# The first chunk's decays spread by one rounded product of stacked high and low rows, with eight blocks of zero products in place of eleven and a new written-out order

## The chip, the cores and the metric

One core of a Trainium2 chip runs the whole program. The metric is the device time of one execution in microseconds (us); less is better. Five engines work side by side, each through its own instructions in a fixed order: TensorE (PE, products), VectorE (DVE), ScalarE (ACT), GpSimd (POOL) and SyncE (SP, which here only issues transfers). An instruction waits for what it reads, and everything behind it on its engine waits with it.

## The reference

Two stages: a gated recurrence over 768 steps (4 batches, 8 heads, chunks of 32 in the reference), and then a gated feed-forward layer over the 3072 rows that it makes.

```python
log_a = np.log(np.clip(a, 1e-06, 1.0))
for c in range(nc):
    cum = np.cumsum(log_a[:, :, sl], axis=-1)
    L = np.exp(cum[:, :, :, None] - cum[:, :, None, :]) * causal
    M = np.einsum('bhin,bhjn->bhij', Cc, Bc) * L
    y[:, :, sl] = M @ x + (C @ state) * exp(cum)
    state = exp(sum) * state + sum_j B_j x_j exp(cum_last - cum_j)
...
gate = 1.0 / (1.0 + np.exp(-(x @ w_gate)))
val = x @ w_val
return (gate * val @ w_out)
```

x has 32 columns for each head and 16 states; the layer goes 256 -> 1536 -> 256. Everything is in 32-bit floats.

## The kernel before

The sequence is cut into six chunks of 128 steps (two halves of 64). For each chunk c the recurrence is a few products: B against C (`pcb`), times the decays, against x (`py`, `mm`), plus the state that came before (`L820`, `L647`). Chunk 0 goes through it batch by batch (`FirstUnit`, four units), since nothing else can be done while the program starts; later chunks go through it in one piece (`Scan`), between the products of the layer. The layer works on the 512 columns of a chunk: `gate` and `value` (`pg`, `pv`, 12 pairs), then `proj` (`po`). Chunks 4 and 5 are done together by a scheme with fewer products (`unit`, `ux`, `uz`, `acc`).

A product of full 32-bit floats takes TensorE several passes. Most of the layer is therefore done on two rounded parts, high and low (`fp32r`), with three products of one pass each; for that each weight tile is first put into a plain form by five instructions on three engines (`split_w`: L482 and L490 on VectorE, L488 and L495 on ScalarE, L497 on GpSimd) and later cut into parts (`part_w`: L513, L515). The first ten of the first chunk's pairs use the full 32-bit weights in their projection, and the first six in their gates as well.

**How the first chunk starts.** `a0` holds the decays of the first 128 steps, one row for each (half, batch, head), 64 rows of 64. VectorE clips them to `ac` and spreads each row over 8 head places (`apart`, a row is zero but in its own head's place; rows 64 to 127 are zero). A product for each unit b with a matrix of zeros and ones (`of_unit[:, b]`, 128 x 128) copies the right row to all 64 partitions of a half (`pa`, L741, `spread`). A running product along each row (L744, the "scan", on VectorE, 512 columns) makes the decays `ab`. Times `pcb` (L691) that is `m` (L695); `m` against x is `py` and `mm` (L706), with the unit's own state sums in the same banks (L716). `sm`, `mr` (L724), `sn` (L848) are the states; `inter`, L820, adds what the first half left to the second. `xw` (L834) takes the result, and `pgv` (L962) are the first layer's products on halves of it.

Ahead of that TensorE multiplies zeros (`warm`, L237): eleven blocks of 128 columns as two products of 512 and one of 384 (`WARM`). `keep_warm` (L289) puts in further products that nobody reads ("fills", 128 columns) where the plan sees TensorE idle in the first 45 us.

**What sets the order.** The program is written as some 300 tasks of several steps. `run()` goes through them with costs for each step (`free`, the numbers in `step(...)`), and picks among the ready steps by a number. Those numbers stand in the table `DUES`, one for each step, 0 to 1246; a letter behind one says which engine takes it (`p` GpSimd, `d` VectorE, `a` ScalarE). So the table sets the order on all engines, and the order of the transfers on SP's queue. `banks` are the three rotating result banks of TensorE (`mm`): a step that takes one waits until the one three turns ago was read out.

Of the kernel before, what the change touches and what calls it, by code (L numbers as in the profile page):

```python
# [8 lines left out]
F32 = mybir.dt.float32  # L9
F32R = mybir.dt.float32r  # L10
# [3 lines left out]
ALU = mybir.AluOpType  # L14
# [121 lines left out]
}  # L136
WARM = (4, 4, 3)
PE0 = 5.6


# [40 lines left out]
def tile_ssd_then_gated_ffn(  # L181
# [11 lines left out]
    nc = tc.nc  # L193
# [4 lines left out]
    P = 128  # L198
# [1283 lines left out]
```

## Time and profile before

| | before |
|---|---|
| median of 3 runs | 345.69 us (345.6 to 346.02) |
| the profiled execution's own time | 345.54 us |
| its span in the trace | 343.7 us |
| TensorE busy | 337.9 us (98%) |
| VectorE, ScalarE, GpSimd busy | 220.2, 150.2, 180.0 us |
| 40.16 MB moved, mean | 117 GB/s |

The span is the time from the first to the last instruction of the trace; the own time, 1.84 us more, has what lies around it. Shares of busy time are means over the whole span; the prediction therefore reads stretches.

### The profile page before, as it was taken

Reading aid. Unit: us, or ns where it says so; the run is one execution under the profiler, and the core shown is the slowest. Engines: PE = TensorE matmul, PEld = TensorE weight load, DVE = VectorE, ACT = ScalarE, POOL = GpSimd, SP = SyncE. Lnnn points to the kernel's source line nnn. Section 1 sums busy time; section 2 is a strip of 40 time slices with the busy share of each in tenths; the row PEclk is TensorE's granted clock in tenths of the full one; section 3 lists DMA queues with packets and bytes.
Section 4 is the critical chain, followed back from the end, with each engine's and each line's share of the span. In section 5 each row is a group of like instructions: output and inputs, shape, how many; then the busy total and the mean of one; then the engine's idle time right before and its main releaser. Section 6 shows DMA issues by size and latency. Waiting matters only on the chain.

```text
span 343.7 us, 7948 instructions
## 1 busy us (share of the span) xinstructions
PE 337.9 (98%) x3144; PEld 261.7 (76%) x3144; DVE 220.2 (64%) x377; ACT 150.2 (44%) x277; POOL 180.0 (52%) x181
## 2 busy tenths in 40 slices
PE   8899999999999999999999999999999999999996
PEld 3474587457888888888888888888888888888885
DVE  5889978956879872456666954566064646856221
ACT  4476987124744230136411513361047557645300
POOL 4646265431646434566774545489427885355500
PEclk9999999999999999999999999999999999999999
DMA  6996899871674376476543621108123733220032
GB/s 107 180 352 209 256 272 146 162 132 35 94 159 62 90 109 159 97 139 89 145 100 102 85 76 21 63 3 297 72 36 91 240 89 110 110 61 2 0 58 67
DMA packets 100247, 40.16 MB, mean 117 GB/s; under 512 B 88754, under 2 KB 91826, under 8 KB 99570
## 3 DMA queue, kind: packets, MB, share of 16 engines
q1 hardware_dynamic: 97906, 39.39, 49.3%
q10 hardware_dynamic: 2304, 0.26, 0.5%
q8 instruction: 25, 0.41, 0.5%
q14 instruction: 12, 0.10, 0.1%
HBM read 30.00 MB, written 9.63 MB: 115 GB/s over the span
## 4 chain that ended last, share of the span: by engine, by line
PE 98%; DVE 1%; ACT 0%; issue 0%
PE pg L981 17%; PE pv L981 17%; PE ux L1121 6%; PE acc L1121 6%; PE po L1017 5%; PE po L1013 5%; PE po L1019 5%; PE po L1018 5%; PE acc L1224 5%; PE uz L1121 5%; PE pg L972 2%; PE pv L972 2%; PE po L1251 2%; PE pcb L706 2%; PE pcb L691 2%; PE pcb L647 2%
## 5 line engine op out<-in xcount | busy, mean ns | idle before, releaser
L981 PE MATMUL pg<-xh,w 128*128 128x512 f32 x168 | 59.0, 392 | 0.0
L981 PE MATMUL pv<-xh,w 128*128 128x512 f32 x168 | 58.9, 391 | 0.0
L927 POOL TENSOR_TENSOR h<-g,h 128x512 fp32r<-128x512 f32 x27 | 38.3, 1420 | 24.4 <-ACT h L925 17.2
L921 DVE TENSOR_TENSOR g<-pv,g 128x512 f32<-128x512 f32 x38 | 26.1, 688 | 30.1 <-PE pv L981 29.1
L903 ACT ACTIVATE g<-pg 128x512 f32<-128x512 f32 x47 | 28.0, 596 | 39.4 <-PE pg L981 37.2
L981 PEld LDWEIGHTS pg<-xh,w 128*128 128x128 f32 x168 | 31.5, 188 | 6.7
L981 PEld LDWEIGHTS pv<-xh,w 128*128 128x128 f32 x168 | 31.5, 188 | 6.6
L497 POOL TENSOR_TENSOR wr<-wr 128x512 int32<-128x512 int32 x18 | 20.5, 1143 | 26.8 <-ACT wr L495 13.0
L981 PE MATMUL pg<-xl,w 128*128 128x512 f32 x84 | 32.7, 389 | 0.0
L981 PE MATMUL pv<-xl,w 128*128 128x512 f32 x84 | 32.7, 389 | 0.0
L1017 PE MATMUL po<-h,w 128*128 128x512 f32 x76 | 30.8, 405 | 0.0
L1019 PE MATMUL po<-h,w 128*128 128x512 f32 x76 | 29.6, 390 | 0.0
L1018 PE MATMUL po<-h,w 128*128 128x512 f32 x76 | 29.6, 389 | 0.0
L577 DVE TENSOR_TENSOR_SCAN ab<-ab,delta 128x512 f32<-128x512 f32 x20 | 28.1, 1424 | 0.0
L925 ACT CAST h<-g 128x512 fp32r<-128x512 f32 x26 | 16.0, 619 | 24.2 <-DVE g L921 24.0
L1048 POOL TENSOR_TENSOR c<-c,c 128x512 f32<-128x512 f32 x13 | 17.2, 1326 | 17.9 <-ACT c L1176 9.2
L1048 POOL TENSOR_TENSOR h<-c,h 128x512 fp32r<-128x512 f32 x16 | 21.0, 1323 | 9.4 <-ACT h L1200 9.3
L1048 POOL TENSOR_TENSOR sw<-sw 128x128 f32<-128x128 f32 x36 | 18.9, 535 | 11.2 <-DVE sw L1048 10.2
L1028 DVE STREAM_TRANSPOSE o<-po 128x256 f32<-128x256 f32 x16 | 6.3, 430 | 21.2 <-PE po L1019 19.2
L1200 ACT CAST h<-c 128x512 fp32r<-128x512 f32 x24 | 14.9, 619 | 10.7 <-POOL c L1048 7.1
L981 PEld LDWEIGHTS pv<-xl,w 128*128 128x128 f32 x84 | 15.8, 188 | 3.2
L981 PEld LDWEIGHTS pg<-xl,w 128*128 128x128 f32 x84 | 15.8, 188 | 3.2
(197 smaller groups left out, 733.2 us busy)
## 6 DMA issues: line engine op xcount, KB each, us to landing
w_s<-sp SPq DMA_DIRECT2D x12, 512.0 KB
s<-w_s SPq DMA_DIRECT2D x12, 512.0 KB
ab<-a_z SPq DMA_DIRECT2D x10, 512.0 KB
wr<-in_moe_w_gate_dram SPq DMA_DIRECT2D x6, 512.0 KB
wr<-in_moe_w_val_dram SPq DMA_DIRECT2D x6, 512.0 KB
wr<-in_moe_w_out_dram SPq DMA_DIRECT2D x6, 512.0 KB
xn<-in_x_dram SPq DMA_DIRECT2D x5, 512.0 KB
out_dram<-o SPq DMA_DIRECT2D x144, 16.0 KB
```

The costliest lines, as they stand in the source:

```text
L497: nc.gpsimd.tensor_tensor(out=lw.bitcast(I32), in0=hw.bitcast(I32), in1=lw.bitcast(I32), op=ALU.add)
L577: nc.vector.tensor_tensor_scan(out=t, data0=t, data1=delta.rearrange("p h l -> p (h l)"), initial=0.0, op0=ALU.mult, op1=ALU.add,)
L903: nc.scalar.activation(gs[k, f], pm, AF.Sigmoid)
L921: nc.vector.tensor_tensor(out=g, in0=pm, in1=g, op=ALU.mult)
L927: engines[eng].tensor_tensor(out=hl, in0=g, in1=hh.bitcast(F32), op=ALU.subtract)
L981: nc.tensor.matmul(pm, w[:, part, kt, fs], xx[:, kt], start=(i == 0), stop=(i == 3 * NK - 1))
L1013: nc.tensor.matmul(acc, whole[NF + f // 2][:, f % 2, ms], hs[k, f], start=start, stop=stop)
L1017: nc.tensor.matmul(acc, hi, hh, start=start, stop=False)
L1018: nc.tensor.matmul(acc, hi, hl, start=False, stop=False)
L1019: nc.tensor.matmul(acc, lo, hh, start=False, stop=stop)
L1048: engines[eng].tensor_tensor(out=out, in0=in0, in1=in1, op=op)
L1121: nc.tensor.matmul(out, a[i], b[j], start=start and n == 0, stop=n == 2, skip_group_check=True)
```

## The change

Four things. (1) `a0` is loaded twice, rows 0 to 63 by SP's queue and rows 64 to 127 by ScalarE's; VectorE rounds all 128 rows to `ah`, and in the lower 64 rows subtracts the rounded value, so that they hold the remainder. `apart` then holds high rows over low rows, `of_unit` has its ones in both halves, and the product of `spread` is one of rounded operands in which the sum over the 128 rows puts high and low together again. GpSimd's clearing of `apart`'s lower half (L1280) is gone. (2) `WARM` is (4, 4): eight blocks. (3) Some steps may now go to another engine: the rounding copy of `part_w` and of `weight_sums` to GpSimd, the picking of `sm` and `mr` in the first chunk to ScalarE. (4) `DUES` is another table, with other planned start costs (`PE0`, `free`, the `spread` step's 0.35 for 1.0).

```diff
-    "": "0 1", "b0": "2", "w0": "3", "b3": "4", "b1": "5", "products0": "6 7 9 13 18", "products0_0": "8 11 28",
...
-WARM = (4, 4, 3)
-PE0 = 5.6
+WARM = (4, 4)
+PE0 = 4.7
...
-        of_b2, eye[:, :R2].rearrange("p (o b h) -> p b o h", o=2, b=NB), axis=mybir.AxisListType.X, op=ALU.add
+        of_b2, eye2.rearrange("p (o b h) -> p b o h", o=2, b=NB), axis=mybir.AxisListType.X, op=ALU.add
...
-    of_unit = hp.tile([P, NB, P], F32, tag="h8", name="of_unit")
+    head2 = const.tile([P, H], F32, name="head")
+    nc.vector.tensor_reduce(head2, eye2.rearrange("p (k h) -> p h k", h=H), axis=mybir.AxisListType.X, op=ALU.add)
+    of_unit = hp.tile([P, NB, P], F32R, tag="h8", name="of_unit")
...
-        free = {"sp": 1.0, "pe": PE0, "act": 3.5, "dve": 5.4, "pool": 4.0, "none": 0.0}
+        free = {"sp": 1.0, "pe": PE0, "act": 3.5, "dve": 4.7, "pool": 4.0, "none": 0.0}
...
-        yield step("act", ACT_SB, needs)
+        eng = yield step(("act", "pool"), (ACT_SB, 0.75), needs)
         hw, lw = halves.pop(i)
         hi, lo = parts_of(i)
-        nc.scalar.copy(hi, hw)
+        copies[eng](hi, hw)
...
+    def chosen_of(eng, out, local):
+
+        if eng == "dve":
+            return chosen(out.rearrange("p (o c) -> p o c", o=1), local.rearrange("p (o c) -> p o c", o=1), 1)
+        for g in range(NG):
+            gs = slice(g * D, (g + 1) * D)
+            nc.scalar.mul(out[:, gs], local[:, gs], of_g[:, g : g + 1])
...
-            yield step("pe", 1.0, [("a0",)], banks=1)
+            yield step("pe", 0.35, [("a0",)], banks=1)
...
-            yield step("dve", 0.21, [], [("first", 0, b)])
+            eng = yield step(("dve", "act"), (0.21, 0.45), [], [("first", 0, b)])
...
-    apart = hp.tile([P, H, L2], F32, tag="h2", name="apart")
-    nc.gpsimd.memset(apart[R2:], 0.0)
-    a0 = hp.tile([R2, L2], F32, tag="h0", name="a0")
+    apart = hp.tile([P, H, L2], F32R, tag="h2", name="apart")
+    a0 = hp.tile([P, L2], F32, tag="h0", name="a0")
     av = a.rearrange("b h s -> (b h) s")
-    nc.sync.dma_start(a0, av[:, :L].rearrange("k (o l) -> o k l", o=2))
+    for r, eng in enumerate((nc.sync, nc.scalar)):
+        eng.dma_start(a0[r * R2 : (r + 1) * R2], av[:, :L].rearrange("k (o l) -> o k l", o=2))
...
+    ah = wk.tile([P, L2], F32R, tag="sp", name="ah", bufs=1)
+    nc.vector.tensor_copy(ah, ac)
+    nc.vector.tensor_tensor(out=ah[R2:], in0=ac[R2:], in1=ah[R2:].bitcast(F32), op=ALU.subtract)
     nc.vector.tensor_tensor(
-        out=apart[:R2], in0=ac.rearrange("p (o l) -> p o l", o=1).broadcast_to([R2, H, L2]),
-        in1=head2.rearrange("p (h o) -> p h o", o=1).broadcast_to([R2, H, L2]), op=ALU.mult,
+        out=apart, in0=ah.bitcast(F32).rearrange("p (o l) -> p o l", o=1).broadcast_to([P, H, L2]),
+        in1=head2.rearrange("p (h o) -> p h o", o=1).broadcast_to([P, H, L2]), op=ALU.mult,
     )
```

The table moves most instructions of the program somewhere; the number of products is the same but for the zero products and the fills. Three places follow as the engines' instructions stand (line, operation, output and inputs by the program's names with buffer numbers, size).

TensorE at the very start, before. `pt` are the transposed B and C of a unit, `pp` the running products that the states need.

```order
L237 MATMUL warm<-warm_sb 128x512 x2
L237 MATMUL warm<-warm_sb 128x384
L756 MATMUL pt_141<-eye,bn_127 128x128
L757 MATMUL pt_141<-eye,cq_129 128x128
L741 MATMUL pa_146<-apart,of_unit 128x512
L871 MATMUL pp_154<-apb,of_row 128x256
L741 MATMUL pa_162<-apart,of_unit 128x512
L741 MATMUL pa_167<-apart,of_unit 128x512
L691 MATMUL pcb_179<-bct_148 64x128 x8
```

The same place after the change.

```order
L234 MATMUL warm<-warm_sb 128x512 x2
L284 MATMUL warm<-eye 128x128
L744 MATMUL pa_141<-apart,of_unit 128x512
L744 MATMUL pa_144<-apart,of_unit 128x512
L759 MATMUL pt_148<-eye,bn_129 128x128
L760 MATMUL pt_148<-eye,cq_131 128x128
L284 MATMUL warm<-eye 128x128 x4
L874 MATMUL pp_161<-apb,of_row 128x256
L686 MATMUL pcb_170<-bct_155 64x128 x8
L284 MATMUL warm<-eye 128x128
```

Two spreads stand ahead of the first transposes now, and fills (`warm<-eye`) between; in the whole first chunk there are 18 fills where 4 were.

VectorE from the first scan to the last `m` of the first chunk, before; `wr_131` is the first gate weight tile (w0), `wr_192` the first value tile (w1).

```order
L744 SCALAR_TENSOR_TENSOR ab_158<-pa_146,delta 128x512
L490 TENSOR_SCALAR wr_131<-wt_160 128x512
L744 SCALAR_TENSOR_TENSOR ab_158<-pa_162,delta 128x512
L744 SCALAR_TENSOR_TENSOR ab_158<-pa_167,delta 128x512
L695 TENSOR_TENSOR m_202<-pcb_179,ab_158 128x512
L744 SCALAR_TENSOR_TENSOR ab_158<-pa_195,delta 128x512
...
L695 TENSOR_TENSOR m_202<-pcb_179,ab_158 128x512 x2
L482 TENSOR_SCALAR wr_192<-wr_192 128x512
L724 TENSOR_TENSOR sm_258<-py_284,mask 128x64
L724 TENSOR_TENSOR mr_327<-mm_228,mask 128x64
L848 SCALAR_TENSOR_TENSOR sn_333<-sm_258,pp_164,mr_327 128x64
L695 TENSOR_TENSOR m_202<-pcb_179,ab_158 128x512
```

After the change (`wr_216` is w1; w0's clip, L482 before, has gone to GpSimd).

```order
L747 SCALAR_TENSOR_TENSOR ab_151<-pa_183,delta 128x512
L747 SCALAR_TENSOR_TENSOR ab_151<-pa_191,delta 128x512
L485 TENSOR_SCALAR wr_133<-wt_195 128x512
L690 TENSOR_TENSOR m_186<-pcb_170,ab_151 128x512
L727 TENSOR_TENSOR sm_275<-py_234,mask 128x64
L690 TENSOR_TENSOR m_186<-pcb_170,ab_151 128x512
L787 TENSOR_TENSOR cd_200<-bct_202,of_q 128x256
L799 TENSOR_TENSOR bd_197<-bn_129,ab_151 128x128
L727 TENSOR_TENSOR sm_275<-py_293,mask 128x64
L782 TENSOR_TENSOR bct_155<-bct_155,pp_179 128x64
L477 TENSOR_SCALAR wr_216<-wr_216 128x512
L690 TENSOR_TENSOR m_186<-pcb_170,ab_151 128x512
```

The clip of w1 still stands ahead of the last `m`, with three short instructions of other engines' work (`cd`, `bd`, `bct`) in front of it, and two `sm` behind fewer `m`.

TensorE at the seventh gate of the first chunk (`pg_6`), before; it is the first that reads the rounded parts of x and of a weight.

```order
L972 MATMUL pg_5_567<-xw_269,wr_340 128x512 x2
L972 MATMUL pv_5_584<-xw_269,wr_335 128x512 x2
L289 MATMUL pg_6_607<-eye 128x128 x3
L981 MATMUL pg_6_607<-xh_372,w_572 128x512
L981 MATMUL pg_6_607<-xl_373,w_572 128x512
L981 MATMUL pg_6_607<-xh_372,w_572 128x512 x2
L981 MATMUL pg_6_607<-xl_373,w_572 128x512
L981 MATMUL pg_6_607<-xh_372,w_572 128x512
L289 MATMUL pv_6_629<-eye 128x128
```

The four fills there are gone in the changed program; the products around them stand as they did. Further on, VectorE's four scans of chunk 1 (L577), which stood one before and three behind the read of the last value bank (`g_11`, L921), stand together ahead of it; and SP's queue takes chunk 1's `pp` loads behind its `bn` and `xn`, not ahead.

## Rows read from the trace of the kernel before

**Rows 1.** TensorE by stretch: us, busy (instructions), granted clock, DMA share, GB/s.

```profile
0.00:24.40 24.40, 21.79 (x337) 1.00 0.88 203
24.40:340.50 316.10, 316.10 (x2809) 1.00 0.48 111
```

**Rows 2.** The chain of waits, first 45 us: start, us, engine and tile.

```profile
1.09 5.04 PE warm L237 x6
...
15.52 0.61 DVE wr L482
...
17.03 0.71 PE py L289 x4
17.74 0.17 PE py L706
...
21.73 2.79 PE pgv L962 x12
24.52 1.72 PE pg L972 x4
...
41.69 0.67 PE pg L289 x6
42.36 1.39 PE pg L981 x6
43.75 0.22 PE pv L289 x2
```

**Rows 3.** VectorE in order of time, first 20 us: start, us, line, operation, tiles.

```profile
3.24 0.23 DVE L1287 TENSOR_SCALAR ac<-a 64x64 f32<-64x64 f32 x1 [0.26 <-DMA a<-in_a_dram]
...
3.63 0.68 DVE L1289 TENSOR_TENSOR apart<-ac,head 64x512 f32<-64x512 f32 x1
...
7.25 1.22 DVE L744 TENSOR_TENSOR_SCAN ab<-pa,delta 128x512 f32<-128x512 f32 x1
...
8.93 2.34 DVE L744 TENSOR_TENSOR_SCAN ab<-pa,delta 128x512 f32<-128x512 f32 x2
...
13.12 0.40 DVE L784 TENSOR_TENSOR cd<-bct,of_q 128x256 f32<-128x256 f32 x1
13.44 0.21 DVE L724 TENSOR_TENSOR sm<-py,mask 128x64 f32<-128x64 f32 x1
14.23 1.29 DVE L695 TENSOR_TENSOR m<-pcb,ab 128x512 f32<-128x512 f32 x2 [0.58 <-PE pcb L691]
15.44 0.68 DVE L482 TENSOR_SCALAR wr<-wr 128x512 f32<-128x512 f32 x1
...
16.62 0.68 DVE L695 TENSOR_TENSOR m<-pcb,ab 128x512 f32<-128x512 f32 x1
```

**Rows 4.** All engines by stretch: PE, PEld, DVE, ACT, POOL busy, clock, DMA share, GB/s.

```profile
6.10:12.00 5.90, 5.67 (x33) 2.16 (x31) 4.86 (x7) 3.44 (x12) 3.15 (x6) 1.00 1.03 115
12.00:14.20 2.20, 1.98 (x86) 1.41 (x88) 1.65 (x4) 1.27 (x7) 1.25 (x5) 1.00 0.83 238
14.20:17.00 2.80, 1.88 (x80) 1.30 (x78) 2.73 (x7) 1.56 (x7) 1.49 (x3) 1.00 1.01 205
```

**Rows 5.** SP's queue in order of time: issue, us that it took.

```profile
10.29 0.94 SPq L468 DMA_DIRECT2D wr<-in_moe_w_val_dram  x1
11.27 1.09 SPq L434 DMA_DIRECT2D xn<-in_x_dram  x2
12.41 2.42 SPq L468 DMA_DIRECT2D wr<-in_moe_w_gate_dram  x1
```

**Rows 6.** VectorE in order of time around the seventh gate.

```profile
41.19 0.68 DVE L890 TENSOR_TENSOR xl<-xw,xh 128x512 fp32r<-128x512 f32 x1
...
42.69 0.69 DVE L515 TENSOR_TENSOR w<-wr,w 128x512 fp32r<-128x512 f32 x1
```

**Rows 7.** VectorE in order of time at chunk 1's scans.

```profile
56.37 0.69 DVE L921 TENSOR_TENSOR g<-pv,g 128x512 f32<-128x512 f32 x1 [0.73 <-PE pv L981]
...
61.13 5.31 DVE L577 TENSOR_TENSOR_SCAN ab<-ab,delta 128x512 f32<-128x512 f32 x3
```

More of the change, by code (lines that the diff above doesn't have):

```diff
@@ L265, in tile_ssd_then_gated_ffn @@
     nc.vector.tensor_reduce(
-        of_b2, eye[:, :R2].rearrange("p (o b h) -> p b o h", o=2, b=NB), axis=mybir.AxisListType.X, op=ALU.add
+        of_b2, eye2.rearrange("p (o b h) -> p b o h", o=2, b=NB), axis=mybir.AxisListType.X, op=ALU.add
     )
-    head2 = const.tile([R2, H], F32, name="head")
-    nc.vector.tensor_reduce(
-        head2, eye[:R2, :R2].rearrange("p (k h) -> p h k", h=H), axis=mybir.AxisListType.X, op=ALU.add
-    )
-    of_unit = hp.tile([P, NB, P], F32, tag="h8", name="of_unit")
+    head2 = const.tile([P, H], F32, name="head")
+    nc.vector.tensor_reduce(head2, eye2.rearrange("p (k h) -> p h k", h=H), axis=mybir.AxisListType.X, op=ALU.add)
+    of_unit = hp.tile([P, NB, P], F32R, tag="h8", name="of_unit")
     nc.vector.tensor_copy(
@@ L293, in tile_ssd_then_gated_ffn @@
     engines = {"dve": nc.vector, "pool": nc.gpsimd}
-    copies = {"dve": nc.vector.tensor_copy, "act": nc.scalar.copy}
+    copies = {"dve": nc.vector.tensor_copy, "act": nc.scalar.copy, "pool": nc.gpsimd.tensor_copy}
     def task(due, name, gen):
@@ L813, in result @@
             own(self.bd, got["xn", 0][:, b], lambda i, rows: py[i][rows, NK])
-            yield step("dve", 0.21, [], [("first", 0, b)])
+            eng = yield step(("dve", "act"), (0.21, 0.45), [], [("first", 0, b)])
             self.s1 = state_of(0, "sm", 1)[:, b]
-            chosen(self.s1.rearrange("p (o c) -> p o c", o=1), py[0][:, NK:], 1)
+            chosen_of(eng, self.s1, py[0][:, NK])
             yield step("pe", 0.32, [("cd", 0, b)], [("inter", 0, b)] + [("inter", 0)] * (b == NB - 1))
@@ L825, in result @@
             self.take(1)
-            yield step("dve", 0.21, [], [("after", 0, b)], banks=-1)
+            eng = yield step(("dve", "act"), (0.21, 0.45), [], [("after", 0, b)], banks=-1)
             if ("mr", 0) not in got:
@@ L829, in result @@
             self.after = got["mr", 0][:, b]
-            chosen(self.after.rearrange("p (o c) -> p o c", o=1), py[1][:, NK:], 1)
+            chosen_of(eng, self.after, py[1][:, NK])
         def take(self, i):
@@ L1062, in weight_sums @@
             sum_up(eng, out, in0, in1, op)
-        yield step("act", ACT_SB)
+        eng = yield step(("act", "pool"), (ACT_SB, 0.7))
         parts = hp.tile([P, 2, 512], F32R, tag="r1", name=f"sp{i}")
-        nc.scalar.copy(parts[:, 0], t[:, 1])
+        copies[eng](parts[:, 0], t[:, 1])
         eng = yield step(("dve", "pool"), (DVE_SB, POOL_SB), port=True)
@@ L1278, in tile_ssd_then_gated_ffn @@
     w_s = dr.tile([NF, P, 2 * 4 * P], F32, name="w_s")
-    apart = hp.tile([P, H, L2], F32, tag="h2", name="apart")
-    nc.gpsimd.memset(apart[R2:], 0.0)
-    a0 = hp.tile([R2, L2], F32, tag="h0", name="a0")
+    apart = hp.tile([P, H, L2], F32R, tag="h2", name="apart")
+    a0 = hp.tile([P, L2], F32, tag="h0", name="a0")
     av = a.rearrange("b h s -> (b h) s")
-    nc.sync.dma_start(a0, av[:, :L].rearrange("k (o l) -> o k l", o=2))
+    for r, eng in enumerate((nc.sync, nc.scalar)):
+        eng.dma_start(a0[r * R2 : (r + 1) * R2], av[:, :L].rearrange("k (o l) -> o k l", o=2))
     az, ap = (hp.tile([NB * H, S], F32, tag=f"h{10 - i}", name=f"a{i}") for i in range(2))
     nc.scalar.activation(table, table, AF.Sigmoid)
-    ac = hp.tile([R2, L2], F32, tag="h11", name="ac")
+    ac = hp.tile([P, L2], F32, tag="h11", name="ac")
     nc.vector.tensor_scalar(out=ac, in0=a0, scalar1=1e-6, scalar2=1.0, op0=ALU.max, op1=ALU.min)
     nc.vector.memset(ac[:, :1], 0.0)
+    ah = wk.tile([P, L2], F32R, tag="sp", name="ah", bufs=1)
+    nc.vector.tensor_copy(ah, ac)
+    nc.vector.tensor_tensor(out=ah[R2:], in0=ac[R2:], in1=ah[R2:].bitcast(F32), op=ALU.subtract)
     nc.vector.tensor_tensor(
-        out=apart[:R2], in0=ac.rearrange("p (o l) -> p o l", o=1).broadcast_to([R2, H, L2]),
-        in1=head2.rearrange("p (h o) -> p h o", o=1).broadcast_to([R2, H, L2]), op=ALU.mult,
+        out=apart, in0=ah.bitcast(F32).rearrange("p (o l) -> p o l", o=1).broadcast_to([P, H, L2]),
+        in1=head2.rearrange("p (h o) -> p h o", o=1).broadcast_to([P, H, L2]), op=ALU.mult,
     )
@@ L1353, in initial @@
         yield step("none", 0.0, [], made)
-        yield step("none", 4.9, [], [("a0",)])
+        yield step("none", 4.7, [], [("a0",)])
     task(-60.0, "", initial())
```

230 rows, old and new, of the table DUES are left out of this document.

## The prediction

> **What bounds the kernel now.** I first read TensorE's busy time by stretch [rows 1]. From 24.4 to 340.5 us it is busy for all 316.10 us, and since the change keeps the number of products, that stretch can only get shorter by what in it is not needed. Before 24.4 it lacks 24.40 - 21.79 = 2.6 us, and part of its busy time there are zero products. Behind 340.5 come 3.2 us of last reads and stores, whose instructions keep their order. So the gain has to come from the first 24 us and from fills.
>
> Then I read the chain of waits [rows 2], to see what the start hangs on. It opens with 5.04 us of zero products on TensorE (from 1.09), and later leaves TensorE for VectorE's clip of a weight tile (15.52) and comes back at 17.03 with two fills; the third unit's products start at 17.74. From 21.73 on it is TensorE alone: the half products `pgv`, and from 24.52 the first full gate. Here the reader should see that TensorE is the bound from about 17 us on, and VectorE and what it waits for ahead of that.
>
> The third view is VectorE in order of time [rows 3]. The clip of the decays starts when they land (3.24), `apart` is done at 3.63 + 0.68 = 4.31, but the first scan starts only at 7.25: TensorE was still on zeros. From there to the end of the last `m`, 16.62 + 0.68 = 17.30, VectorE works nearly without a break.
>
> **The change part by part.**
>
> *The warm-up and the spread.* Eleven zero blocks took 5.04, so eight take 3.67 and end at 4.76. The one fill behind them costs a block at that pace, 0.46: TensorE can take the first spread at 5.22. `apart` must be there: two more instructions on 64 columns, each at most the 0.23 of the clip on the same columns [rows 3], move it from 4.31 to 4.77 at the latest, and GpSimd's clearing falls away. The second half of the load goes by ScalarE's queue, which has nothing else to do; it may be 0.45 late before anything notices. A product of rounded operands, one pass, is in the rows as six in 1.39, 0.23 each; the full one is 1.72 for two, 0.86 [rows 2]. That is at the fast clock. [...] So the first rounded spread costs 0.46, ends near 5.7, and the first scan starts near 5.75 instead of 7.25. The four spreads together go from 3.44 to some 1.4 us of TensorE; the fills that come in (18 for 4) fill time in which it would wait, and cost at most 0.22 each where it would not.
>
> The zero blocks and fills in the rows show the lower level for all the zeros and the higher one from the transposes at about 6 us on; the granted-clock column says 1.00 even for the first stretch [rows 1], so I go by the durations. [...]
>
> *What VectorE has to do.* From first scan to last `m`: four scans at 2.34 / 2, four `m` at 1.29 / 2, w0's second pass and w1's clip at no more than 0.68 each, and two `sm`, `cd` and two small ones that came over from GpSimd at no more than 0.40 each [rows 3]: 4.7 + 2.6 + 1.4 + 2.0 = 10.7, or about 9.4 with the short ones at half that. Before it was 17.30 - 7.25 = 10.05. The work alone would let the last `m` end at 5.75 + 9.4 = 15.2, two us sooner.
>
> *What the data allow.* But the last `m` stands behind w1's clip, and the third unit needs its x. From 6.1 to 17 the transfers fill the queues: shares 1.03, 0.83, 1.01 [rows 4]. SP issued w1 (512 KB) at 10.29, the last two `xn` (256 KB together) at 11.27, then w2, whose issue took 2.42 [rows 5]. The bytes fit: 2.2 us at 238 GB/s are w1's half megabyte, so w1 is there by about 14.3 to 15.4 (its clip began at 15.44, which is the latest), and 256 KB at 205 GB/s more take 1.25, so x is there by about 15.6 to 16.5. The change takes no bytes from ahead of these; it adds 16 KB. I take 15.0 and 16.0. Then the clip ends at 15.6 and the last `m` at 16.3, 1.0 sooner than 17.30; the third unit's products can start at 16.0, 1.7 sooner than 17.74.
>
> *To the full gates.* From 17.74 to 24.52 TensorE did 6.78 us of work that stays. Started at 16.0 it would end at 22.8; the last `m` and the clip of w2 ahead of the last `sm` (w2 lands behind x) push that back. I take 1.3, between 1.0 and 1.7: the first full gate starts near 23.2. The bounds: 0, if x lands only when it was used before (17.74), and 2.2, if it is there at 15.6. GpSimd's clip of w0 appears in no row for that engine; between the 0.68 of VectorE and the 3 us until ScalarE needs it nothing later moves, because the data wait is behind it.
>
> *The seventh gate.* Of the four fills there (0.67 + 0.22 [rows 2]) none is left: 0.89 less. They covered a real wait in part: the low half of x was ready at 41.19 + 0.68 = 41.87, the weight of the value product at 42.69 + 0.69 = 43.38 [rows 6], while TensorE without fills would have come at 41.69 and about 43.3. In the new order VectorE makes the low half of x before the half products are even read, and the weight parts stand behind the same gate's read as before, which itself moves up. So I take 0.89; if the old waits stay, 0.6.
>
> *Elsewhere.* Two rounding copies of weights and two of sums go to GpSimd, two `mr` to ScalarE. Nothing waits for them in TensorE before, and GpSimd is idle for half of the span; I cost them at nothing. If their cover goes, a copy is 1 us late once.
>
> Sum: 345.54 - 1.3 - 0.89 = 343.35 for an execution like the profiled one. That one is 0.15 under the median of the runs (345.69), so I forecast 343.5.
>
> **The rivals.**
>
> *The start gives nothing back.* x and w1 land as late as they were used. Then only the fills of the seventh gate are gone: 345.69 - 0.9 = 344.8. For it: the queues are full all through [rows 4]. Against: TensorE lacked 0.92 us in 14.2 to 17.0 and VectorE was busy for 2.73 of 2.80, so it was work, not data, that was late there.
>
> *The new order makes waits that eat the gain.* After 24.4 there was none; the table moves almost everything. One wait of 1.5 to 2.5 us, or several short ones, gives 345.0 to 346.2. For it: hardly a row keeps its neighbours. Against: VectorE, ScalarE and GpSimd have a third to a half of their time free.
>
> [...]
>
> *Slower: chunk 1's scans.* VectorE does all four in one piece ahead of the read of the last value bank. Before, three took 5.31 [rows 7], so four take up to 7.1. TensorE has two quarter projections (8 products of 0.86, 6.9) and chunk 1's own `pcb` until it needs that bank, so there is about 1 us in hand. The decays come by a broadcast load whose landing no row shows, and in the new order the first scan is wanted at about 56.37 + 0.69 + 0.8 - 2.2 = 55.7. If it lands 1 us late nothing happens; at 3.9 us late the whole gain (2.2 + 0.7) is gone and it becomes slower, by what comes on top: 347. Against: the scans waited for no transfer before.
>
> **How the numbers follow.** Forecast as summed: 0.58, with its own range 342.6 (2.2 at the start) to 344.4 (0.6 at the start, 0.6 at the seventh gate). Start gives nothing, 344.8: 0.12. Waits eat it, 345.0 to 346.2: 0.14. Clock, 343.9: 0.04. Slower, 347: 0.12. Faster by over 0.2% (under 345.0; 0.2% is about what a measurement of this kernel can tell from no change) are the first, second and fourth: 0.74. Same 0.14, slower 0.12. The range for 8 in 10 goes from 342.6 up to 345.3, which takes in the forecast, the two mild rivals and a little of the waits.
>
> **What would show it.** First scan near 5.75; TensorE's six-product records at the seventh gate with no L289 row ahead; the first full gate at 23.2, and the first half products of chunk 0 moved by the same; `py` of the third unit near 16.0 behind a wait for a transfer; and from there TensorE busy without a gap to about 338.3. It is wrong if a TensorE wait of over 0.5 us stands anywhere behind 24 us, if the first full gate starts after 24.0, or if zero-like products keep their 0.46 beyond 6.5 us.

## The result, and the profile after

| | before | changed |
|---|---|---|
| time, median of 6 runs | 345.74 us (345.33 to 346.02) | 348.46 us (346.95 to 349.94) |
| ratio, 95% interval | | 1.008 (1.0056 to 1.0104) |
| the profiled execution: its time, its span | 345.54, 343.7 | 349.94, 348.1 |
| first scan on VectorE starts | 7.25 | 6.14 |
| first full gate starts, in the order of time | 24.36 | 26.41 |
| TensorE's last product ends | 340.50 | 343.98 |

The change made the kernel 0.8% slower, and its runs spread over 3 us where those of before lie within 0.7. The profiled execution of the changed kernel is the slowest of its six, so its 4.4 us over before are more than the 2.7 us between the medians.

The waits of TensorE are where I look first. Rows: who waited for what, us in total, times, longest.

```profile
PE py L284 <- issue: 1.3, 1, 1.3
PE pgv L965 <- DMA wr<-in_moe_w_val_dram: 1.1, 1, 1.1
PE warm L234 <- DVE warm_sb L231: 1.1, 1, 1.1
PE pcb L686 <- DVE sm L727: 0.8, 1, 0.8
PE pg L984 <- DVE g L924: 0.8, 1, 0.8
```

Three of these are new: a stop with no releaser ("issue") at the third unit's fills, one ahead of a half product that is put down to a weight's transfer, and one at a gate. They stand here in the order of time on TensorE (start, duration, instructions, idle time ahead).

```profile
15.82 0.45 PE L823 MATMUL mm<-cd,sm 128*64 128x64 f32 x8
16.20 0.38 PE L284 MATMUL py<-eye 128*128 128x128 f32 x1
17.93 0.94 PE L284 MATMUL py<-eye 128*128 128x128 f32 x7 [1.35 <-issue]
...
22.20 0.45 PE L823 MATMUL mm<-cd,sm 128*64 128x64 f32 x8
23.74 1.11 PE L965 MATMUL pgv<-xw,wr 128*128 128x256 f32 x4 [1.09 <-DMA wr<-in_moe_w_val_dram]
...
25.98 0.59 PE L965 MATMUL pgv<-xw,wr 128*128 128x256 f32 x2
26.41 1.02 PE L975 MATMUL pg<-xw,wr 128*128 128x512 f32 x2
```

A product of full 32-bit floats stands in the trace as two MATMUL records, two passes (a rounded one as one: the four spreads are 8 records before and 4 in the changed kernel). The first stop splits a zero product into its two: the first pass ran at 16.20, the second at 17.93. The second pass has no operand that the first hadn't, so no data was waited for. The second stop is at an instruction that waits for a semaphore; the last transfer that this semaphore counts had landed by 22.82, and TensorE went on at 23.64, so the wait view's releaser is not what ended it.

Against before the 4.4 us of the profiled executions are made up of: the first full gate 2.05 later; from there to the seventh gate's value product 0.82 less (18.55 for 19.37; the fills are gone); from there to TensorE's end 2.25 more (299.02 for 296.77; 0.94 of it at 106.5 us, 0.86 spread over the small products `pcb<-ab,xn` of L701, the rest in pieces); and 0.93 more behind TensorE's end (4.09 for 3.16).

VectorE at the start, as in [rows 3]:

```profile
3.66 0.26 DVE L1290 TENSOR_SCALAR ac<-a 128x64 f32<-128x64 f32 x1 [0.69 <-DMA a<-in_a_dram]
3.98 0.06 DVE L1291 MEMSET ac<- 128x1 f32 x1
4.07 0.19 DVE L1293 CAST ah<-ac 128x64 fp32r<-128x64 f32 x1
4.30 0.22 DVE L1294 TENSOR_TENSOR ah<-ac,ah 64x64 fp32r<-64x64 f32 x1
4.56 0.69 DVE L1295 TENSOR_TENSOR apart<-ah,head 128x512 fp32r<-128x512 f32 x1
...
6.14 2.34 DVE L747 TENSOR_TENSOR_SCAN ab<-pa,delta 128x512 f32<-128x512 f32 x2 [0.58 <-PE pa L744]
```

The spread that the first scan waits for, on TensorE:

```profile
5.31 1.22 PE L744 MATMUL pa<-apart,of_unit 128*128 128x512 f32 x2
```

What the change does at the start works: the scans begin 1.1 us sooner. The gain is lost behind it, on TensorE.

What stops TensorE is seen by counting. These are TensorE's products (PE) and weight loads (PEld) in two stretches, from the start to the first stop and between the stops (columns: stretch, its length, busy time, instructions in it, granted clock, DMA share, GB/s).

```profile
0.00:16.58 16.58, 14.69 (x219) 1.00 0.82 135
17.92:22.43 4.51, 4.50 (x127) 1.00 0.86 241
...
0.00:16.58 16.58, 9.75 (x220) 1.00 0.82 135
17.92:22.43 4.51, 3.65 (x126) 1.00 0.86 241
```

With TensorE's own semaphore instructions (10 up to there) the first stop stands ahead of its 450th record and the second one exactly 256 records on. The transfers have a queue of their own kind for instructions; whole span, then 15 to 16 us, then 20 to 22 us:

```profile
q8 instruction: 25, 0.41, 0.5%
...
q8 instruction: 1, 0.02, 7.0%
...
q8 instruction: 1, 0.02, 4.2%
```

25 packets of 16 KB for the 6,371 records of TensorE come to 64 bytes a record, so by this estimate one packet is 256 records, as many as stand between the two stops. The trace's packets put the two fetches at 15.35 to 16.48 and 21.04 to 22.38; TensorE goes on at 17.93 and 23.64, 1.45 and 1.26 us after each. In the trace of before the fetch ends at 16.77, and there too TensorE stops at the same record, from 17.79 to 18.12, without a semaphore. So my first theory: **instructions come in blocks of 256, and TensorE stands still at a border between two blocks when it gets there before the next has come.** Records are counted from 0 below, so the borders are records 449, 705, 961 and so on. The rival is what the wait view says: **transfers**, a weight that lands late because SP issues small loads ahead of it.

### The profile page after: what moved, and what is told of

It is laid out like the page before. It is cut to its first block, busy times and chain, and to the rows that moved or that the text cites. A ratio compares the mean times of both kernels' runs of the same rounds, so it can differ in the third digit from the quotient of the medians.

```text
span 348.1 us, 7964 instructions
## 1 busy us (share of the span) xinstructions
PE 338.9 (97%) x3158; PEld 264.3 (76%) x3158; DVE 226.5 (65%) x385; ACT 145.5 (42%) x271; POOL 177.0 (51%) x181
## 4 chain that ended last, share of the span: by engine, by line
PE 87%; SPq 5%; DMA 4%; DVE 2%; issue 1%; ACT 0%; ACTq 0%; DVEq 0%
PE pg L984 16%; PE pv L984 16%; PE ux L1124 6%; PE acc L1124 5%; PE po L1020 5%; PE po L1016 5%; PE po L1021 5%; PE po L1022 5%; PE uz L1124 5%; PE acc L1227 4%; PE pv L975 2%; PE pg L975 2%; PE pcb L701 2%; DMA out_dram<-o 2%; SPq L426 2%; DMA wr<-in_moe_w_val_dram 2%
## 5 line engine op out<-in xcount | busy, mean ns | idle before, releaser
L930 POOL TENSOR_TENSOR h<-g,h 128x512 fp32r<-128x512 f32 x23 | 31.8, 1385 | 30.0 <-ACT h L928 19.9
L924 DVE TENSOR_TENSOR g<-pv,g 128x512 f32<-128x512 f32 x38 | 26.1, 686 | 19.7 <-PE pv L984 15.3
L928 ACT CAST h<-g 128x512 fp32r<-128x512 f32 x27 | 16.6, 619 | 33.2 <-DVE g L924 33.2
L1051 POOL TENSOR_TENSOR h<-c,h 128x512 fp32r<-128x512 f32 x18 | 24.2, 1354 | 9.8 <-ACT h L1203 9.7
L572 DVE TENSOR_TENSOR_SCAN ab<-ab,delta 128x512 f32<-128x512 f32 x20 | 26.3, 1352 | 0.0
L1051 POOL TENSOR_TENSOR sw<-sw 128x128 f32<-128x128 f32 x36 | 17.2, 492 | 11.2 <-DVE sw L1051 10.5
L1031 DVE STREAM_TRANSPOSE o<-po 128x256 f32<-128x256 f32 x16 | 6.3, 431 | 23.2 <-PE po L1022 23.1
L510 POOL TENSOR_TENSOR w<-wr,w 128x512 fp32r<-128x512 f32 x7 | 9.9, 1419 | 16.3 <-ACT w L508 12.8
```

Source lines behind the costliest of these rows:

```text
L572: nc.vector.tensor_tensor_scan(out=t, data0=t, data1=delta.rearrange("p h l -> p (h l)"), initial=0.0, op0=ALU.mult, op1=ALU.add,)
L924: nc.vector.tensor_tensor(out=g, in0=pm, in1=g, op=ALU.mult)
L930: engines[eng].tensor_tensor(out=hl, in0=g, in1=hh.bitcast(F32), op=ALU.subtract)
L1051: engines[eng].tensor_tensor(out=out, in0=in0, in1=in1, op=op)
```

## The experiments

Twelve kernels, 4 to 11 runs each. The starts are those of the order of time, as in the table above; "stops" are breaks of over 0.25 us between two starts on TensorE that stand at a border and are longer than the same step takes elsewhere. A break of 0.32 at record 4034 (the changed kernel, w_first, old_fills) is not one: it is the step from a long product to the burst of L701, and that step takes 0.32 in the kernel before too, at 121.2, 141.3, 188.3 and 213.4 us, where no border is.

| run | first full gate | seventh gate | TensorE's end | span | median, ratio to before (95%) | stops at records (us) |
|---|---|---|---|---|---|---|
| before | 24.36 | 42.12 | 340.5 | 343.7 | | 449 (0.33) |
| changed | 26.41 | 43.18 | 344.0 | 348.1 | 348.46, 1.0056 to 1.0104 | 449 (1.62), 705 (1.21) |
| no_fills | 26.55 | 43.31 | 348.0 | 351.1 | 351.78, 1.0152 to 1.0208 | 4289 (1.87), 5057 (2.17) |
| wide_fills | 23.88 | 40.65 | 343.3 | 346.4 | 348.12, 1.0055 to 1.0085 | 4289 (0.27), 5057 (1.43) |
| tiny | 29.36 | 46.12 | 353.1 | 356.2 | 357.94, 1.0325 to 1.0395 | 449 (0.75), 1729 (1.89), 2753 (1.36), 3521 (1.84) |
| w_first | 25.46 | 42.22 | 342.5 | 346.5 | 347.92, 1.005 to 1.0093 | 449 (1.20), 705 (0.38) |
| before_128 | 24.60 | 46.24 | 357.4 | 360.5 | 361.71, 1.0439 to 1.0497 | 1729 (1.51), 2753 (1.92), 3521 (2.07), 4545 (1.93), 5313 (1.59) |
| before_32 | 24.54 | 43.51 | 341.9 | 345.0 | 346.70, 1.0026 to 1.0056 | none over 0.25 |
| wide_48 | 24.10 | 42.52 | 342.5 | 346.3 | 348.15, 1.0058 to 1.0127 | none behind 24 us |
| spread_only | 25.65 | 43.41 | 341.8 | 344.9 | 346.99, 1.0031 to 1.0073 | none behind 24 us |
| wide_cut | 24.23 | 41.05 | 341.5 | 345.4 | 347.01, 1.0031 to 1.0058 | 449 (0.42) |
| wide_cut_dve | 23.89 | 40.72 | 340.3 | 344.2 | 345.71, 1.0003 to 1.0023 | 449 (0.66) |
| old_fills | 24.05 | 40.82 | 339.9 | 343.0 | 345.01, 0.9977 to 1.0009 | none |
| tail | 23.64 | 41.72 | 343.7 | 346.8 | 346.77, 1.0024 to 1.0051 | none |

**no_fills.** The changed kernel without its zero products of the first chunk.

```diff
-        for _ in range(int(FILL * idle[0] / FILL_T + (0.9 if first_y[0] else MORE))):
+        for _ in range(0):
```

> The changed kernel without its 18 zero products of the first chunk (72 of TensorE's records: a weight load and a product for each of two passes). Two theories for its two stops, 16.58 to 17.93 and 22.43 to 23.74. Instructions: TensorE's instructions come from memory in blocks of 256; the 449th and the 705th record stand at these stops in the changed kernel, and each goes on 1.26 to 1.45 us after a fetch of 16 KB has landed. Then without the fills some 50 records more of useful work stand ahead of the first stop and 72 ahead of the second; the stops stand at the same record numbers, 449 and 705, at other products, and the first full gate starts at 24.5 to 25.7 instead of 26.58; 346.5 to 347.8 us. Transfers: the stop before the half products is the wait for a weight that lands late; the fills take no time from that, the wait stays in front of the same product, and the first full gate starts at 26.3 to 26.7; 348 to 349 us.

Neither came. There is no stop at 449 or 705, but the first full gate is as late as before the edit, because TensorE was slow all the way to it. Products of the same shape between 5 and 24.5 us, first in the changed kernel and then without fills (count, busy, mean ns):

```profile
L686 PE MATMUL pcb<-bct 32*64 32x128 f32 x64 | 1.9, 292 | 0.8 <-DVE sm L727 0.8
L759 PE MATMUL pt<-eye,bn 128*128 128x128 f32 x4 | 1.3, 316 | 0.0
```

```profile
L686 PE MATMUL pcb<-bct 32*64 32x128 f32 x64 | 2.9, 442 | 0.1
L759 PE MATMUL pt<-eye,bn 128*128 128x128 f32 x4 | 1.8, 445 | 0.6 <-ACT bct L769 0.6
```

So it is the fills that bring the clock to its upper level this early: the trace's first clock record, at the upper level, stands at 23.75 us without them and at 6.44 in the changed kernel. And two stops of 1.87 and 2.17 us appear at 189 and 214 us, far from the edit: in the small `pcb` products of chunks 4 and 5, at records 4289 and 5057, both borders. Leaving out 72 records at the start had moved every later border in the program.

**wide_fills.** The same zero columns, in fewer instructions.

```diff
+        n = int(FILL * idle[0] / FILL_T + (0.9 if first_y[0] else MORE))
+        while n:
+            r = min(n, 4, to.shape[-1] // P)
+            nc.tensor.matmul(to[:, : r * P] ..., eye, eye ... .broadcast_to([P, r, P]), start=start, stop=True)
+            n -= r
```

> The changed kernel with the same columns of zero products in the first chunk, but each group of two to four as one product of up to 512 columns: the same work for TensorE with some 40 records fewer, about 30 of them ahead of the first stop. Instructions: the stops stand at records 449 and 705 again, at products that come later in the program, and the first full gate starts 0.4 to 1.2 us earlier than 26.58. Transfers: nothing changes, 26.3 to 26.7.

The instructions theory's direction, and more than its size: the first full gate comes at 23.88, 2.5 us sooner than in the changed kernel and 0.5 sooner than before. Of the stops at the start 0.2 us is left. The time hardly moved (348.12), because later borders now fall into bursts (1.43 at 209.6 us).

**tiny.** 16 small products at a place where TensorE waits.

```diff
             keep_warm(self.pcb[:, 0])
+            if b == 3:
+                for _ in range(16):
+                    nc.tensor.matmul(warm[:32, :64], eye[:32, :32], eye[:32, :64], start=True, stop=True)
```

> The changed kernel with 16 more products of 32x32 by 64 columns (64 records, some 0.3 us of TensorE) put ahead of the second half of the first pcb products, where TensorE waits 0.5 to 0.9 us anyway. Instructions: the stops come 64 records earlier in the program; the first one starts near 15 and still ends near 18, and the first full gate starts 0.5 to 1.5 us later than 26.58; 348.7 to 350 us. Transfers: the first full gate within 0.3 of 26.58.

9.5 us slower than the changed kernel, where 0.2 to 1.5 was expected, for two reasons that I had not seen: TensorE's granted clock fell to 0.50 from 14.36 to 24.60, so this run says nothing of the two stops at the start; and three stops in bursts together took 5.1 us, each at a border (64 records further up in the program than without the edit). TensorE's waits there:

```profile
PE pcb L642 <- issue: 4.4, 3, 1.7
```

**w_first.** SP issues the second and third weight tile ahead of the small loads of B and C (DUES numbers of `w2`, `w3` and of the `bq1` and `cq1` loads around them exchanged; `w4` and `w5` move up as well). The edit also ends the fills at 24 us (`COLD` 24 for 45); TensorE's products are 3,158 records with it and without.

> The changed kernel with the loads of the second and third weight tile issued by SP ahead of the four small loads of the next chunk's B and C that stand before them. Instructions: the stops stay at records 449 and 705 and the first full gate starts at 26.0 or later; if the fetch itself is slowed by other transfers, the stops may move by up to 0.5 us. Transfers: the weight lands 1 to 2 us earlier, the stop before the half products is gone or under 0.3 us, and the first full gate starts at 25.4 or earlier; 347 us or less.

Between the two. The stops stay at records 449 and 705, which a late weight would not explain, but they shrink to 1.20 and 0.38: the second fetch of instructions now runs from 20.27 to 21.22 instead of 21.04 to 22.38. So transfers count, but as what the fetch stands among. The traces say more of that: the first packet starts between 14.69 and 15.35 in all fourteen, though TensorE passed the border before it (record 193) anywhere from 11.83 to 13.45. In the changed kernel that is 3.5 us behind the border, with a DMA share of 1.00 in between; in the bursts of before_128, further down, the packets start 0.8 to 1.3 us behind theirs. That the full queues hold the packet back is the likely reading; apart from w_first no run tests it.

**before_128 and before_32.** If borders are the cause, the kernel before is merely lucky in where they fall, and a shift must show it. I fitted one rule to the six traces (the next block is ready 3.8 us after the record that stands 48 ahead of the last border), and laid it over the trace of before, with borders moved by some number of records.

```diff
         keep_warm(pm)
+        if (k, f, j) == (0, 2, 0):
+            for _ in range(32):   # 8 in before_32
+                nc.tensor.matmul(pm[:32, :64], eye[:32, :32], eye[:32, :64], start=True, stop=True)
```

> The kernel before, with 32 products of 32x32 by 64 columns (128 of TensorE's records, some 0.3 us) written into the third gate's bank ahead of its own first product, near 33 us; nothing else is moved. Blocks of instructions: every later border between two blocks of 256 records falls 128 records earlier in the program. Let the next block be ready 3.8 us after the record that stands 48 ahead of the border before (fitted to the six traces so far); laid over the trace of before, that gives five stops of 1.7 to 2.0 us inside the bursts of small pcb products near 80, 124, 143, 191 and 216 us, 9.2 us together: 354.3 to 356.0 us. If the bursts are not bound by instructions: 345.9 to 346.4 us, the work of the added products alone.

> As the run with 128 records, with 8 products, 32 records. Blocks of instructions: the same model gives no stop at all for borders moved by 32; 345.6 to 346.1 us. If it were the added products themselves, or code that is moved in memory, that cost anything, a quarter of what the run with 128 shows.

Five stops, in the five bursts named, 9.0 us together where the rule gave 9.2, and none with 32 records. Counted over all fourteen traces behind 24 us: at the twelve borders where the block and the 48 records ahead of it went by in under 3.0 us TensorE stopped, for 0.27 to 2.17 us; at the other 305, where they took 3.77 or more, it never did. The waits, and one of the stops with what stands around it:

```profile
PE pcb L647 <- issue: 7.9, 5, 1.9
```

```profile
129.24 0.30 PE L647 MATMUL pcb<-ct,sn 32*64 32x64 f32 x8
129.35 0.22 PE L647 MATMUL pcb<-ct,sm 32*64 32x64 f32 x1
131.27 0.34 PE L647 MATMUL pcb<-ct,sm 32*64 32x64 f32 x7 [1.71 <-issue]
```

It stands between the first and the second of eight equal products on the same operands. Between the ends of two such stops (85.44 and 131.27) there are four blocks, 1,024 records. The time was some 6 us more than expected (and that of before_32 0.6), because two prices were wrong: the small products took 0.12 to 0.15 us each (3.9 us for 32 and 1.2 for 8, by the way from first to seventh gate), and behind two of the five stops the granted clock fell to its lower level:

```profile
153.70:157.00 3.30, 3.30 (x11) 0.50 0.02 5
204.90:208.20 3.30, 3.30 (x9) 0.50 1.25 141
```

**wide_48 and wide_cut.** The same rule gave borders clear of all bursts for wide fills with 48 more records. First as 12 small products, then for no added work, by cutting products in two.

```diff
+            cut = 2 if f < 4 else 1
+            for hs_ in range(cut):
+                cs = slice(hs_ * 512 // cut, (hs_ + 1) * 512 // cut)
                 for kt in range(NK):
-                    pm, whole[...][:, kt, fs], xw[0][:, kt], ...
+                    pm[:, cs], whole[...][:, kt, fs], xw[0][:, kt, cs], ...
```

> The changed kernel with wide fills, and 12 products of 32x32 by 64 columns (48 records) ahead of the third gate's own products. Blocks of instructions: the two stops of the run with wide fills (0.3 near 187 and 1.4 near 211 us) go, since both borders move out of the bursts; 1.2 to 2 us less than that run, 346.0 to 346.9 us. Otherwise: 348.1 to 348.6 us.

> The changed kernel with wide fills, whose 12 products of the second to fourth full gates are each made as two of 256 columns: the same columns, 48 records more, and no added product, unlike the run with 48 records, whose 12 small products took 1.65 us. Blocks of instructions: no stop in the bursts behind 44 us, seventh gate at 40.6 to 41.0, TensorE's end 300 us behind it, 344.9 to 346.2 us. If the added records as such cost time (weight loads that don't hide behind half as many columns): the seventh gate at 41.5 or later, 346.5 or more.

Both have no stop in a burst. From the seventh gate to TensorE's end they take 300.0 and 300.5 where wide_fills took 302.6. In wide_48 the 12 products cost 1.7 us on the way to the seventh gate and took the gain back (348.15, a time that the rival had forecast as well, so the trace and not the time decides); the cut ones cost nothing (16.82 from first to seventh gate; 16.77 in wide_fills), and 347.01 is 1.1 less than wide_fills. Both times lie above what I expected; in wide_cut the wait at 106.5 us and the end remain.

**wide_cut_dve.** Rows of the changed kernel, TensorE, VectorE and then GpSimd, around TensorE's wait at 106.5:

```profile
107.70 0.50 PE L984 MATMUL pg<-xh,w 128*128 128x512 f32 x1 [0.78 <-DVE g L924]
...
103.02 1.46 DVE L928 CAST h<-g 128x512 fp32r<-128x512 f32 x1
104.51 2.53 DVE L930 TENSOR_TENSOR h<-g,h 128x512 fp32r<-128x512 f32 x2
106.97 0.68 DVE L924 TENSOR_TENSOR g<-pv,g 128x512 f32<-128x512 f32 x1
...
102.88 1.31 POOL L510 TENSOR_TENSOR w<-wr,w 128x512 fp32r<-128x512 f32 x1 [3.43 <-PE pg L984]
104.15 1.47 POOL L1051 TENSOR_TENSOR sw<-w 128x512 f32<-128x512 f32 x1
105.70 2.06 POOL L1051 TENSOR_TENSOR sw<-sw 128x128 f32<-128x128 f32 x3
```

```diff
-    ... "part16": "424a 434p", ...
+    ... "part16": "424a 434d", ...
...
-    ... "sums0": "444 453 455 ...", ...
+    ... "sums0": "444d 453 455 ...", ...
```

> As the run before it, with the subtraction of the last weight tile and the first sum behind it moved from GpSimd to VectorE, where GpSimd ran 102.88 to 107.8 us in the changed kernel while VectorE's cast took 1.46 (median 0.43) and its two subtractions 1.26 each (median 0.69), and TensorE waited 1.16 between two starts at 106.5. If it is GpSimd that slowed VectorE: the wait at the ninth gate of chunk 1 is gone, 0.7 to 1.0 us less than the run with the cut products. If VectorE was late by its own work: the wait stays or grows, since VectorE gets two more instructions.

The wait is gone and the median is 1.3 us lower (345.71). In the profiled executions 0.92 of that stands behind the seventh gate; the other 0.3 stands at the start, ahead of the edit, and is not its doing. VectorE was given two more instructions and became faster, since its cast takes 0.43 and its two subtractions 1.29 together with GpSimd's subtraction and sum gone from beside them:

```profile
100.84 0.43 DVE L936 CAST h<-g 128x512 fp32r<-128x512 f32 x1
101.30 1.29 DVE L938 TENSOR_TENSOR h<-g,h 128x512 fp32r<-128x512 f32 x2
102.51 0.69 DVE L518 TENSOR_TENSOR w<-wr,w 128x512 fp32r<-128x512 f32 x1
```

The trace of the changed kernel has more of both kinds. The cast (L928) took 0.42 to 0.43 in the five cases with no GpSimd instruction beside it, and 1.02 and 1.46 in the two with one for over 90% of its time; the subtraction (L930) took 0.68 to 0.69 in the six without and 0.92 to 1.79 in six with. The read of a value bank (L924) took 0.66 to 0.69 either way, so not all of VectorE's work is slowed; why the one kind is, no row shows.

**spread_only and old_fills.** The lines of the change for `head`, `of_unit`, `a0`, `ac`, `ah` and `apart` alone, in the old order on every engine; then, as a diff to that, with eight blocks of zeros, without the fills at the seventh gate, and with six wide zero products by hand.

```diff
-WARM = (4, 4, 3)          COLD 45.0
+WARM = (4, 4)             COLD 24.0   # no fills at the seventh gate
+FILLS = {1: 1, 3: 2, 4: 4, 6: 2, 7: 2, 9: 1}
```

> The kernel before with the rounded spread alone: stacked high and low rows, one rounded product for each unit; eleven blocks of zeros, the old order on every engine and the old number of fills. The sum of the prediction: with the blocks of zeros kept, TensorE comes to the spread as late as before; the four spreads are 2.0 us shorter, the second to fourth scans come sooner where they waited for theirs; the first full gate 0.5 to 1.0 us sooner, 344.7 to 345.3 us. Instructions: record 449 can't start before its block is there, near 18.0 as before (18.12), so the first full gate stays within 0.3 us of 24.5 and the time within 345.3 to 346.0 us.

> The kernel before in its old order, with the rounded spread, eight blocks of zeros, no fills at the seventh gate, and in the place of the time that the rounded spreads save on TensorE six wide zero products (28 blocks of 128 columns less than four full spreads took). Clock: the granted clock stays at the upper level from 7 us on, unlike the rounded spread alone, where it was at the lower from 9.3 to 19.5. Instructions: record 449 starts at 18.0 to 18.3 again and holds the first full gate to 24.1 to 24.6; without the fills the seventh gate starts 16.9 behind it, 41.0 to 41.5; from there as before (298.4 to TensorE's end): 344.4 to 345.1 us. If the start were set by VectorE and the transfers as in the prediction: first full gate near 23.2, 343.5 us.

The rounded spread alone made the first full gate 1.3 us later. Its windows on TensorE say why:

```profile
6.00:9.28 3.28, 2.48 (x24) 1.00 1.10 114
9.28:19.50 10.22, 9.43 (x213) 0.50 1.00 239
```

Both expectations for spread_only missed. Four full spreads had kept TensorE busy (3.28 of these 3.28 us in the kernel before, at a clock of 1.00); with rounded ones it is idle for 0.8 of 3.28 us, and then the granted clock is at its lower level, 0.50, for ten. With the six wide fills the clock stays up, the first full gate starts at 24.05, the seventh at 40.82, and the median of 11 runs is 345.01, as the instructions theory had it, against 345.5: 0.1% less, which the interval can't tell from no change. Record 449 started at 17.68, somewhat sooner than forecast. Some of the gain is lost at the seventh gate: 1.10 us pass there between two starts that stand 0.23 apart elsewhere, with a wait for the low half of x, whose old times [rows 6] has.

**tail.** ScalarE at the end of the changed kernel:

```profile
338.34 0.37 ACT L1266 COPY o<-po 128x256 f32<-128x256 f32 x1 [2.87 <-DMA out_dram<-o]
338.40 5.30 ACTq L1041 DMA_DIRECT2D out_dram<-o  x8
343.74 0.65 ACT L1266 COPY o<-po 128x256 f32<-128x256 f32 x2 [5.03 <-DMA out_dram<-o]
```

Eight writes of 5.3 us stand between a copy and the last two, which TensorE had made possible 1 us sooner. I put that copy behind the writes (`proj5_2`: 1225 and 1227 to 1238 and 1240).

> As the run with cut products and VectorE's subtraction, with one move at the end: ScalarE's third-last copy, which stands ahead of its last eight writes of the output and waits for TensorE, goes behind them. If those writes, which then come 3.9 us late, are what the last two copies wait for: the copies follow TensorE's products, the span ends 3.0 to 3.3 us behind TensorE instead of 4.0, 344.8 to 345.2 us, as fast as the kernel before or up to 0.2% faster. If the writes themselves were late (their transfers or SP's): no change, 345.5 to 345.9 us.

The end came as expected (3.1 us behind TensorE instead of 4.0), and the time did not: the copy also frees a bank, and TensorE now waits for that bank.

```profile
PE po L1273 <- DVE o L1280: 1.9, 1, 1.9
```

The profiled execution is the slowest of its six (348.62) and has waits of 0.3 and 0.6 us before the seventh gate besides. Nor does the end prove the reading: in no_fills, wide_fills and tiny, with the copy in its old place, the span ends 3.1 us behind TensorE too, because there the same eight writes took 3.7 us. In wide_fills:

```profile
337.70 3.72 ACTq L1049 DMA_DIRECT2D out_dram<-o  x8
```

So the 0.93 us at the end hang on how long ScalarE's writes take, which differs between executions of one order (5.2 in w_first); why stays open.

## Why the prediction was wrong, point by point

- **The warm-up and the spread**: right in kind, first scan 6.14 for 5.75. The second half of the decays landed 0.42 later by ScalarE's queue than the whole had, and `apart` was done at 5.25; but the fill ahead of the spread ran to 5.28, and the spread started at 5.31, for 5.22 forecast. So most of the 0.39 is the spread itself: the scan began 0.83 behind its start, where I took 0.5. The 0.46 for this spread was my estimate, the 0.23 of a rounded product doubled since a zero block took 0.46 and a fill 0.22 [rows 2]; no run shows it as such. The two spreads start 0.59 apart, and the first one's record runs from 5.31 to 6.10.
- **What VectorE has to do, what the data allow**: the last `m` ended at 17.02 instead of 16.3 (17.30 before), w1's clip began at 15.64 after a wait of 0.20 for the tile (I took 15.0). A miss of 0.7 us. My sum of VectorE's work with the short ones at half is 9.7 and not 9.4; from first scan to last `m` it took 10.9. The third unit's x, taken at 16.0, landed at 17.66 in this execution (by the semaphore that its products wait for). Before it was 15.98; in the experiments with the changed kernel's order it was 15.35 to 15.76, but 16.98 in tail.
- **To the full gates** is the step that failed: "From 17.74 to 24.52 TensorE did 6.78 us of work that stays. Started at 16.0 it would end at 22.8." The 6.78 us are about right (6.69 from 17.19 to 23.88 in wide_fills); the start at 16.0 and the way without a stop are wrong. TensorE was at the third unit's fills at 16.20, near the forecast, and at its products at 18.80: the stop at record 449 took 1.62 of that and the four fills 0.98. The second stop, at record 705, took 1.21 more, and the first full gate came 3.2 us behind the forecast 23.2. Record 449 runs before 17.2 in none of these kernels, whatever stands ahead of it (17.26 to 19.20; 17.93 and 18.12 in the changed kernel and before). In the profiled execution of before, TensorE came to that border just as it opened, so it left no wait that I could have taken for one: 0.33 us inside the small products, and 0.01 in before_128 and before_32, which run the same instructions up to there and whose packet landed 0.5 us sooner. The border is not the only limit at the start: with x at 17.66 the products could not have begun before that here, so some 1.1 us is what the border adds to them beyond that wait. In wide_fills they start at 17.19 behind their fills, with x there since 15.67, and the first full gate comes 0.5 us sooner than before, not 1.3.

```profile
16.14 1.13 PE L287 MATMUL py<-eye 128*128 128x512 f32 x2
17.19 0.24 PE L709 MATMUL py<-m,xn 64*32 64x64 f32 x1
```

- The fills that come in, "at most 0.22 each", were priced as columns. Each is four records, 18 of them 72, more than a quarter of a block, ahead of or between the two borders. Whether the third unit would have started sooner without its four fills no run shows: in no_fills TensorE ran at its lower level.
- **The seventh gate**: right. 0.82 for 0.89.
- **Elsewhere, at nothing**: wrong twice. GpSimd is idle for half of the span (busy 177.0 of 348.1 us), as I had said, but where the new order runs it beside VectorE's cast and subtractions it makes them slow (1.46 for 0.43; 0.94 us of TensorE's time in the profile); and the end took 0.93 more in the profiled execution, though not in every run of this order.
- **The rivals.** "The new order makes waits that eat the gain" was the nearest, but I had thought of waits for data, and of its three new waits two are for instructions. The clock's 343.9, at 0.04, had no row behind it, and no run shows the delay that it stands for: in the changed kernel the granted clock rose at 6.44 us, 0.45 later than before. When the change's own first part stands alone, the clock rises at 5.86 and falls again at 9.28. In the changed kernel it stays at the upper level from 6.44 on, with the fills in, at the price above. Chunk 1's four scans cost TensorE nothing: no wait stands there.
- Two of the prediction's own signs of being wrong came: the first full gate after 24.0, and a wait of over 0.5 us behind it (0.78 at 107 us).

In medians: 348.46 for the changed kernel, 347.01 with fewer records at the start and the borders clear of the bursts (wide_cut), 345.71 with VectorE freed of GpSimd too (wide_cut_dve).

Together these edits take back the loss against before (2.75 us of 2.72). How it divides over the two causes the medians don't show exactly, since a profile is one execution and the first two edits act at the start and in the bursts at once. The gain of 2.2 that was forecast is not there either: the border holds part of the start, and from the seventh gate to TensorE's end the new order takes 299.5 us in wide_cut_dve, where before took 298.4. Three things stay open: the 0.86 us spread over L701, the longer writes at the end, and what makes the runs of the changed kernel differ by 3 us. The last fits stops whose ends hang on when a transfer lands (the third unit's x landed anywhere from 15.35 to 17.66 in executions of this order), but no two profiled executions of the changed kernel were compared.

## What to carry to other kernels

Count TensorE's instructions, not only its columns. Where small products run at some 7 ns a record, a border between blocks cost 0.3 to 2.2 us in these runs whenever the last 304 records had gone by in under 3 us, and nothing where they had taken 3.8 or more; and any instruction added or taken away upstream moves all later borders: an edit in the first 24 us cost 4 us at 189 and 214 (no_fills). A comparison of two versions should list stops without a releaser by their record number before it argues over data, and then look at when the data landed as well: here one of the two came late at the same place. Fill waiting time with few wide products (first full gate at 23.88 in wide_fills, 26.41 in the changed kernel), and move borders by cutting a long product in two (16.82 us from first to seventh gate in wide_cut, 16.77 without the cuts).

## What the runs showed that I had not expected

The stop at a border: 16 KB land, and TensorE goes on 1.2 to 1.7 us later, which in the bursts, for the stops of over 1 us, is 3.1 to 4.0 us after the border before. The granted clock can fall to 0.50 again long after the start, behind a stop in a burst (153.7 us), and so a stop can cost twice; behind the other three stops of before_128 and the two of no_fills it did not. A product of a 32x32 weight with 64 columns took 0.12 us when 32 of them followed one another on the same place, while in the bursts of `pcb` products (32x64 weights, placed in turn) one starts every 0.015 us or so (64 in 0.94 us); that the place makes the difference is not shown.
